# A group's four sums kept on one engine, one more group by seven products, and a small copy cut in 24

## The chip, the cores and the metric

The kernel runs on one core of a Trainium2 chip. A core has five engines that work side by side and wait for one another through semaphores: TensorE (PE) multiplies 128x128 tiles into PSUM, VectorE (DVE) and ScalarE (ACT) read PSUM and SBUF, GpSimd (POOL) works in SBUF, and SyncE (SP) issues most of the DMAs. The metric is the device time of one execution in microseconds (us). A difference of 0.2% (0.5 us here) is about what a measurement of this kernel can tell from no change.

## What is computed

`x` is 2 x 4000 x 512, everything in bfloat16. Two convolutions of five taps, each with a GELU and each keeping every second step, bring 4000 steps to 1000. Then follows the joint network:

```python
fe = jnp.einsum("btd,de->bte", f, w_f)      # 2 x 1000 x 512
ge = jnp.einsum("bud,de->bue", g, w_g)      # 2 x 8 x 512
j = jnp.tanh(fe[:, :, None, :] + ge[:, None, :, :])
return jnp.einsum("btud,dv->btuv", j, w_o)  # 2 x 1000 x 8 x 512
```

The last line is the large one: 16000 rows of `j`, each 512 long, times a 512 x 512 matrix.

## The kernel before

All work is first written down as a list of operations (`Plan.op`, `Plan.dma`), each with what it reads and writes. From overlaps of these the waits follow. Which engine runs which operation in which order is not computed in the kernel: the tables `ORDER["pe"]`, `["act"]`, `["dve"]`, `["pool"]` and `["sp"]` hold it, as differences between operation numbers. Each engine goes through its table from front to back, so an operation that has to wait holds up all that stands behind it on its engine. For some operations (`flex`) the table also decides the engine, which is whichever table holds the number.

The joint stage, from about 130 us to the end, cuts the 16000 rows into 125 tiles of 128 rows. `tanh` (ACT, L453) writes the rows of `j` into two rings, `jT` and `jX`. A tile is multiplied in one of two ways.

- `Plain`: four matmuls of 512 columns, one copy out of PSUM by ACT or DVE, one store.
- `Seven`: four neighbouring tiles are one group, taken as a 2x2 matrix of blocks times the 2x2 blocks of `w_o`, by Winograd's form of Strassen's scheme with seven block products in place of eight. A product is four matmuls of 256 columns, so a group has 28. Beforehand `sums` (L1094) makes four 128x512 sums of blocks of `j` in SBUF, numbered 0 to 3: sum 1 reads sum 0, and sum 3 reads sum 1. Products 5, 6, 7 and 3 use sums 0, 1, 2 and 3. Afterwards seven passes over PSUM bring the result out: three `keep` copies to SBUF (`sn`, L563 on ACT or L564 on DVE), three adds of a kept copy to PSUM, always on DVE (`og`, L448), and one copy `out4` (`og`, L563 or L564). The keep of product 1 must be done before product 6 goes to the same bank, and the add of product 7 before product 4 does.

The loop over `seven` puts products of two groups between each other: product 1 of group n, 7 of n-1, 5 and 2 of n, 6 of n, 4 of n-1, 3 of n. The sums of group n+1 are listed between 2 and 6. Of 125 tiles 28 groups take 112; 13 are `Plain`: two at the start, three at the end, and four pairs in gaps between later groups (`gaps`), each tile of a pair standing between two groups.

In the tables of before, the sums are split one by one: of 112 sums, 86 stand in POOL's table and 26 in DVE's. Twenty of 28 groups have at least one on DVE, none has all four there. `Plan.emit` adds one more kind of wait for these: an operation marked `port` on POOL waits for the nearest earlier marked one on DVE, where the planned starts lie within 1.5 us.

Two small things elsewhere matter. `NPRE` = 14 tiny ACT activations of one number (`warm`, L453) stand at the head of ACT's table; after them come ACT's first copies, of transposed input into `eo`. The first direct matmuls read `eo` and the first tap of `w1`; the following ones need the second tap from HBM. And `ge` (L1004 in the schedule) multiplies `g` by `w_g` into 64 columns of one bank, which a single ACT copy brings to `geT`; every tanh reads one column of it as its bias.

Of the kernel before, what the change touches and what calls it, by code (L numbers as in the profile page):

```python
# [7 lines left out]
ACT = mybir.ActivationFunctionType  # L8
# [6 lines left out]

ORDER = {
    "pe": """
# [13 lines left out]
        4 2 3""",  # L31
    "act": """
# [9 lines left out]
        3 12 7 1 8 1""",  # L42
    "dve": """
# [9 lines left out]
        7 6 17 67 -61 18 -37 46 35 -29 4 17 36 -10 3 -36 13 16 27 7 -21 27 15 -3 9 8 2""",  # L53
    "pool": """
        1 55 1 -55 1 1 1 28 218 1 -217 258 -252 253 8 89 174 150 1 54 -2 1 -31 33 33 2 -1 38 -36 35 40 -38 37 34 2 33
        -32 33 32 -30 31 1 1 33 1 28 1 1 28 155 -154 1 27 2 -1 33 -31 32 1 28 2 -1 31 -29 30 1 26 37 -36 37 1 1 33 34
        -33 34 -32 33 1 29 2 -1 33 2 -1 33 2 -1 35 2 -1 36 2 -1 28 -26 27 1 27 1 27 1 1""",
    "sp": """
        6 15 1 1 1 1 1 1 1 1 1 1 1 2 2 1 1 1 1 2 1 1 1 1 1 248 1 1 1 1 1 1 2 1 1 1 1 1 254 1 1 145 3 33 33 4 1 1 30 4 33
        4 1 1 33 4 31 4 1 1 29 4 29 4 1 1 29 4 25 4 1 1 25 4 25 4 1 1 27 4 27 4 1 1 25 4 25 4 1 1 19 1 11 4 21 11 4 19  # L60
        11 4 17 11 1 1 4 17 11 1 1 4 17 11 4 1 1 19 11 4 21 1 11 4 25 4 23 1 1 4 23 4 19 1 1 7 3 3 5 5""",
}


class View:


    __slots__ = ("ap", "cells", "psum")
# [42 lines left out]


class Op:
    __slots__ = ("eng", "fn", "reads", "writes", "dma", "signal", "count", "sem", "val", "idx", "cost", "pin", "after", "wire", "alt", "port", "slack")


class Plan:
# [12 lines left out]
    def op(self, eng, fn, reads=(), writes=(), cost=0.1):  # L130
        o = Op()
        o.eng, o.fn, o.dma, o.signal, o.idx, o.alt, o.port = eng, fn, False, False, len(self.ops), None, self.port
        o.reads, o.writes, o.cost, o.pin, o.after = tuple(reads), tuple(writes), cost, self.pin, list(self.hold)
        self.ops.append(o)
        return o
# [7 lines left out]
    def dma(self, eng, fn, reads=(), writes=(), sem=None, nbytes=524288, rate=330e3, slack=0.0):  # L143

        o = Op()
        o.eng, o.fn, o.dma, o.signal, o.idx, o.alt, o.port = eng, fn, True, False, len(self.ops), None, False
        o.reads, o.writes, o.cost, o.pin, o.after, o.wire = tuple(reads), tuple(writes), 0.43, True, [], nbytes / rate
        o.slack = slack
        if sem is None:
            sem = [self.nc.alloc_semaphore(f"s_d{o.idx}"), 0]  # L150
        sem[1] += 16
        o.sem, o.val = sem[0], sem[1]
        self.ops.append(o)
        return o
# [162 lines left out]
def bass_standalone__seq2seq_rnn_t_joint__speech_kernel(  # L317
# [22 lines left out]
    NK = D // P  # L340
# [12 lines left out]
    BU = B * U  # L353
    NT = 512
    NWARM = 8
    NPRE = 14
    TAPS = (0, 4, 2, 1, 3)
    NX = 2

    with ExitStack() as es:  # L360
        cur = [16512]
# [32 lines left out]
        geT = at("geT", [NK * BU], FP32)  # L394
# [3 lines left out]
        warm = at("warm", [2], FP32)  # L398
# [36 lines left out]
        ps = Psum(es.enter_context(nc.psum_tensor("acc", [P, 8 * NT], FP32)))  # L435
        block = es.enter_context(nc.Block(no_gpsimd_drain=True))
        pl = Plan(nc)
        sub, add = ALU.subtract, ALU.add
# [12 lines left out]
        def act(o, i, func, scale=1.0, bias=None):  # L451
            rd = (i,) if bias is None else (i, bias)
            pl.op("act", lambda e: e.activation(o.ap, i.ap, func, scale=scale,  # L453
                                                bias=0.0 if bias is None else bias.ap), rd, (o,),
                  o.ap.free_size() * 0.833e-3 + (0.05 if i.psum else 0.105 if bias is None else 0.186))
# [42 lines left out]
            return pl.dma("sp", lambda e: e.dma_start_transpose(out=dst.ap, in_=src), (), (dst,), nbytes=n * 2 * D, rate=175e3, slack=slack)  # L498

        came = [load_xr(0)]  # L500
        for _ in range(NPRE):
            act(warm[0:1], warm[1:2], ACT.Gelu_apprx_tanh)

        def load_w1(i, after=None):
            o = load_w("sp", w1_sb[i], w1[i].rearrange("(k c) d -> c k d", c=P), 0.5 if i == TAPS[1] else 0.2)
# [196 lines left out]
        class Unit:  # L702


            count = 0
# [108 lines left out]
        def ge():  # L814
            c0 = bank()
            for m in range(NK):
                mm(ps.cols(c0 + m * BU, BU), [(wg_sb[k, m * P:(m + 1) * P], gT[k]) for k in range(NK)], True, True)
            act(geT[:], ps.cols(c0, NK * BU), ACT.Copy)

        def fe(b, half, m):  # L820
            q = NT3 // 2
# [250 lines left out]
        class Seven:  # L1072
# [15 lines left out]
            def sums(self):  # L1088
                S = self.S
                eng = "dve" if self.n in (0, 1) else "pool"  # L1090
                pl.port = True
                for i, x, y, op in ((0, self.a(1, 0), self.a(1, 1), add), (1, S[0], self.a(0, 0), sub),
                                    (2, self.a(0, 0), self.a(1, 0), sub), (3, self.a(0, 1), S[1], sub)):
                    fn = lambda e, o=S[i], x=x, y=y, op=op: e.tensor_tensor(out=o.ap, in0=x.ap, in1=y.ap, op=op)  # L1094
                    alt = {"pool": (fn, 1.12), "dve": (fn, 0.34)}
                    pl.flex({k: alt[k] for k in (("dve", "pool"))}, (x, y), (S[i],))
                pl.port = False

            def product(self, i, bk, start, check=False):
# [125 lines left out]
        piece(4)  # L1225

        S1 = 15
        gaps = (1, 3, 5, 7)
        jts = [2 + 4 * i for i in range(S1)]
        j = 2 + 4 * S1  # L1230
        for n in range(13):
            jts.append(j)
            j += 4 + 2 * gaps.count(n)
        assert jts[-1] + 4 < ntile
# [72 lines left out]
```

## Time and profile before

| what | value |
|---|---|
| time, median of 3 runs | 250.3 us (250.1 to 250.35) |
| profiled execution, its own time | 250.55 us |
| its span | 248.7 us |
| PE busy in the span | 243.8 us (98%) |
| DVE busy | 208.0 us (84%) |
| ACT busy | 197.6 us (79%) |
| POOL busy | 100.7 us (41%) |
| granted clock of TensorE | 1.00 |

The span is what the profiler sees of the engines; the time holds 1.85 us more that lie around it. Matmuls overlap one another, so the pace of PE is read from the starts of neighbouring matmuls and not from the duration of one. An engine that is busy for 80% of the whole span can be full in one stage; the table by stage, below, shows which.

### The profile page before, as it was taken

Reading aid. Unit: us, or ns where it says so; the run is one execution under the profiler, and the core shown is the slowest. Engines: PE = TensorE matmul, PEld = TensorE weight load, DVE = VectorE, ACT = ScalarE, POOL = GpSimd, SP = SyncE. Lnnn points to the kernel's source line nnn. Section 1 sums busy time; section 2 is a strip of 40 time slices with the busy share of each in tenths; the row PEclk is TensorE's granted clock in tenths of the full one; section 3 lists DMA queues with packets and bytes.
Section 4 is the critical chain, followed back from the end, with each engine's and each line's share of the span. In section 5 each row is a group of like instructions: output and inputs, shape, how many; then the busy total and the mean of one; then the engine's idle time right before and its main releaser. Section 6 shows DMA issues by size and latency. Waiting matters only on the chain.

```text
span 248.7 us, 5271 instructions
## 1 busy us (share of the span) xinstructions
PE 243.8 (98%) x1938; PEld 182.6 (73%) x1944; DVE 208.0 (84%) x371; ACT 197.6 (79%) x349; POOL 100.7 (41%) x107
## 2 busy tenths in 40 slices
PE   7999999999999999999999999999999999999994
PEld 3879976666666666666566888777788878777883
DVE  1799996967999994796957889778999999996793
ACT  8787948458786475643699999999999999998672
POOL 1000000000000000000008988978799999999530
PEclk9999999999999999999999999999999999999999
DMA  6999999989000061000001043323345554454547
GB/s 212 319 224 179 126 209 173 193 169 355 31 3 0 0 209 48 0 4 0 0 3 42 31 147 106 100 87 127 109 156 161 172 188 162 160 182 137 192 153 249
DMA packets 54871, 31.83 MB, mean 128 GB/s; under 512 B 31902, under 2 KB 54590, under 8 KB 54846
## 3 DMA queue, kind: packets, MB, share of 16 engines
q1 hardware_dynamic: 54558, 31.34, 47.2%
q8 instruction: 15, 0.25, 0.5%
q10 hardware_dynamic: 288, 0.16, 0.2%
q14 instruction: 10, 0.08, 0.1%
HBM read 7.60 MB, written 16.38 MB: 96 GB/s over the span
## 4 chain that ended last, share of the span: by engine, by line
PE 86%; ACT 7%; DMA 2%; issue 1%; DVE 1%; SPq 0%; DVEq 0%; ACTq 0%
PE acc L461 86%; ACT jT L453 3%; DMA w_sb<-in_w_dram 2%; ACT sn L563 1%; ACT og L563 1%; ACT jX L453 1%; DVE og L448 1%; ACT sd L453 1%; DVE sn L564 0%; DVE og L564 0%; PE acc L599 0%; ACT fT L453 0%; SPq L479 0%; SPq L488 0%; ACT ost L453 0%
## 5 line engine op out<-in xcount | busy, mean ns | idle before, releaser
L448 DVE TENSOR_TENSOR og<-acc,sn 128x512 bf16<-128x512 f32 x84 | 54.7, 682 | 5.1 <-PE acc L461 5.1
L453 ACT ACTIVATE jT<-feT,geT 128x1000 bf16<-128x1000 f32 (+5 forms) x60 | 57.5, 1017 | 0.3 <-DVE feT L448 0.3
L1094 POOL TENSOR_TENSOR ss<-jT 128x512 f16<-128x512 bf16 x34 | 39.7, 1182 | 35.2 <-DVE ss L1094 33.3
L461 PE MATMUL acc<-tw,ss 128*128 128x256 f16 x336 | 46.0, 273 | 0.0
L461 PE MATMUL acc<-row,w_sb 128*128 128x334 bf16 (+2 forms) x224 | 39.2, 297 | 0.0
L461 PEld LDWEIGHTS acc<-tw,ss 128*128 128x128 f16 x336 | 32.3, 98 | 7.5 <-ACT sn L563 0.5
L461 PE MATMUL acc<-wo_sb,jT 128*128 128x256 bf16 (+1 forms) x205 | 33.1, 283 | 0.2
L563 ACT ACTIVATE sn<-acc 128x512 f32<-128x512 f32 x48 | 29.7, 628 | 3.4 <-PE acc L461 2.8
L564 DVE COPY sn<-acc 128x512 f32<-128x512 f32 x36 | 24.6, 685 | 6.3 <-PE acc L461 6.0
L453 ACT ACTIVATE hT<-acc 128x334 bf16<-128x334 f32 (+3 forms) x36 | 15.4, 430 | 17.4 <-PE acc L461 16.9
L461 PEld LDWEIGHTS acc<-row,w_sb 128*128 128x128 bf16 x224 | 21.2, 97 | 9.3 <-DVE acc L605 0.7
L453 ACT ACTIVATE sd<-acc 128x334 f32<-128x334 f32 (+2 forms) x48 | 20.5, 432 | 8.7 <-PE acc L461 7.4
L461 PEld LDWEIGHTS acc<-wo_sb,jT 128*128 128x128 bf16 x208 | 20.2, 98 | 5.1
L1094 POOL TENSOR_TENSOR ss<-ss,jT 128x512 f16<-128x512 f16 x19 | 22.3, 1179 | 2.4 <-DVE ss L1094 1.9
L445 POOL MEMSET hT<- 128x8 bf16 (+2 forms) x6 | 0.8, 148 | 55.5 <-ACT hT L453 43.0
L448 DVE TENSOR_TENSOR row<-row 128x1336 bf16<-128x1336 bf16 (+2 forms) x24 | 19.1, 806 | 0.0
L1094 POOL TENSOR_TENSOR ss<-jT,ss 128x512 f16<-128x512 bf16 x15 | 17.5, 1169 | 2.4 <-DVE ss L1094 2.4
L453 ACT ACTIVATE jX<-feT,geT 128x1000 bf16<-128x1000 f32 (+3 forms) x20 | 18.4, 965 | 0.0
L605 DVE SCALAR_TENSOR_TENSOR acc<-acc,sd 128x334 f32<-128x334 f32 (+2 forms) x24 | 11.7, 488 | 7.6 <-PE acc L461 7.5
L461 PE MATMUL acc<-xp,w_t 128*128 128x334 bf16 (+1 forms) x96 | 17.6, 305 | 0.0
L461 PE MATMUL acc<-hT,w_t 128*128 128x334 bf16 x96 | 17.6, 304 | 0.0
L461 PE MATMUL acc<-wo_sb,ss 128*128 128x256 bf16 x112 | 17.1, 273 | 0.0
(129 smaller groups left out, 473.4 us busy)
## 6 DMA issues: line engine op xcount, KB each, us to landing
out_dram<-og SPq DMA_DIRECT2D x42, 256.0 KB, 2.2
w_sb<-in_w_dram SPq DMA_DIRECT2D x10, 512.0 KB, 5.9
out_dram<-og SPq DMA_DIRECT2D x14, 128.0 KB, 2.3
out_dram<-ost SPq DMA_DIRECT2D x10, 128.0 KB, 1.9
xr<-in_x_dram SPq DMA_DIRECT2D x1, 512.0 KB, 3.2
wf_sb<-in_w_f_dram SPq DMA_DIRECT2D x1, 512.0 KB, 4.2
wg_sb<-in_w_g_dram SPq DMA_DIRECT2D x1, 512.0 KB, 5.2
wo_sb<-in_w_o_dram SPq DMA_DIRECT2D x1, 512.0 KB, 6.8
```

The lines of the kernel that those rows point to most:

```text
L445: pl.op("pool", lambda e: e.memset(v.ap, 0.0), (), (v,))
L448: pl.op(eng, lambda e: e.tensor_tensor(out=o.ap, in0=a.ap, in1=b.ap, op=op), (a, b), (o,), 0.02 + 2.14e-3 * o.ap.free_size() if eng == "po ...
L453: pl.op("act", lambda e: e.activation(o.ap, i.ap, func, scale=scale, bias=0.0 if bias is None else bias.ap), rd, (o,), o.ap.free_size() * ...
L461: ins = e.matmul(o.ap, lhsT=l.ap, rhs=r.ap, start=start and n == 0, stop=stop and n == len(pairs) - 1, skip_group_check=not check)
L563: pl.flex({"act": (lambda e: e.activation(o.ap, v.ap, ACT.Copy), 0.05 + n * 0.833e-3), "dve": (lambda e: e.tensor_copy(out=o.ap, in_=v.ap) ...
L564: "dve": (lambda e: e.tensor_copy(out=o.ap, in_=v.ap), 0.065 + n * 1.04e-3)}, (v,), (o,))
L605: pl.op(eng, lambda e: e.scalar_tensor_tensor(out=o.ap, in0=a.ap, scalar=f, in1=b.ap, op0=ALU.mult, op1=add), (a, b), (o,), vec_cost(o, (a ...
L1094: fn = lambda e, o=S[i], x=x, y=y, op=op: e.tensor_tensor(out=o.ap, in0=x.ap, in1=y.ap, op=op)
```

## The change

- `sums` no longer splits a group. Groups 0, 1, 4, 7, 10, 13, 16, 19, 22 and 25 (`ONV`) have all four sums on DVE, the other groups all four on POOL. The order within a group becomes 0, 2, 1, 3. On DVE the first sum also lists the other inputs of the group among its reads, so the group starts when all its data is there. (`glue` is set and read nowhere.)
- 29 groups in place of 28. They take 116 tiles, and 9 are `Plain`: two at the start, three at the end, two pairs in gaps.
- Thirteen of the 14 tiny activations go.
- The copy of `ge` to `geT` becomes 24 copies of two or three columns each.
- All five tables are new. From their running sums: the operations on PE go from 696 to 706, on ACT from 350 to 363, on DVE from 371 to 385, on POOL from 103 to 93, on SP from 138 to 137. DVE has 40 sums in place of 26, POOL 76 in place of 86. The copies that either engine could take go, on ACT, from 82 to 83 (keeps 51 to 58, `out4` 24 to 20, plain tiles 7 to 5; the keeps and outs of the second convolution's projection are counted in), on DVE from 47 to 46 (39 to 35, 4 to 9, 4 to 2). PE's table is the same through the tail; in the joint stage product 1 of the next group now often stands before product 4 of the last. The 24 pieces stand on ACT between the two last `fT` evictions before the joint stage (22 of them) and right behind (2). In DVE's table the blocks of four of seven groups are unbroken; in groups 7, 10 and 22 there stand 8, 13 and 19 other operations among the four. The blocks of groups 13, 16, 19 and 25 have the add of a product 7 right behind them.

```diff
-    NPRE = 14
+    ONV = (0, 1, 4, 7, 10, 13, 16, 19, 22, 25)
     TAPS = (0, 4, 2, 1, 3)
     NX = 2
+    NG = 24
...
-        for _ in range(NPRE):
-            act(warm[0:1], warm[1:2], ACT.Gelu_apprx_tanh)
+        act(warm[0:1], warm[1:2], ACT.Gelu_apprx_tanh)
...
-            act(geT[:], ps.cols(c0, NK * BU), ACT.Copy)
+            cut = [NK * BU * i // NG for i in range(NG + 1)]
+            for i, j in zip(cut, cut[1:]):
+                act(geT[i:j], ps.cols(c0 + i, j - i), ACT.Copy)
...
-                for i, x, y, op in ((0, self.a(1, 0), self.a(1, 1), add), (1, S[0], self.a(0, 0), sub),
-                                    (2, self.a(0, 0), self.a(1, 0), sub), (3, self.a(0, 1), S[1], sub)):
+                for i, x, y, op in ((0, self.a(1, 0), self.a(1, 1), add), (2, self.a(0, 0), self.a(1, 0), sub),
+                                    (1, S[0], self.a(0, 0), sub), (3, self.a(0, 1), S[1], sub)):
                     fn = lambda e, o=S[i], x=x, y=y, op=op: e.tensor_tensor(out=o.ap, in0=x.ap, in1=y.ap, op=op)
-                    alt = {"pool": (fn, 1.12), "dve": (fn, 0.34)}
-                    pl.flex({k: alt[k] for k in (("dve", "pool"))}, (x, y), (S[i],))
+                    if self.n in ONV:
+                        o = pl.op("dve", fn, (x, y) if i else (x, y, self.a(0, 0), self.a(0, 1)), (S[i],), 0.34)
+                        o.glue = i > 0
+                    else:
+                        pl.op("pool", fn, (x, y), (S[i],), 1.12)
...
-        gaps = (1, 3, 5, 7)
+        gaps = (1, 5)
         jts = [2 + 4 * i for i in range(S1)]
         j = 2 + 4 * S1
-        for n in range(13):
+        for n in range(14):
             jts.append(j)
             j += 4 + 2 * gaps.count(n)
```

More of the change, by code (lines that the diff above doesn't have):

```diff
@@ L17 @@
     "pe": """
[2 rows of a table removed]
[2 rows of a table added]
         1 -9 1 12 1 5 1 23 1 4 1 2 1 2 1 6 2 1 4 1 2 1 2 1 2 2 1 4 1 2 1 2 1 16 2 1 4 1 2 1 2 1 18 2 1 4 1 2 1 2 1 18 2
         1 4 1 2 1 2 1 14 2 1 4 1 2 1 2 1 10 2 1 4 1 2 1 2 1 5 2 1 4 1 2 1 2 1 6 2 1 4 1 2 1 2 1 2 2 1 4 1 2 1 2 1 6 7 1
[2 rows of a table removed]
[2 rows of a table added]
         2 6 1 2 1 3 1 3 1 4 1 2 1 2 1 2 1 2 1 8 1 2 1 3 1 5 1 6 1 2 1 2 1 2 1 2 1 6 1 2 1 3 1 3 6 1 2 1 2 1 2 1 2 6 1 2
         1 3 1 5 4 1 2 1 2 1 2 1 2 6 1 2 1 3 1 3 4 1 2 1 2 1 2 1 2 6 1 2 1 3 1 5 4 1 2 1 2 1 2 1 2 6 1 2 1 3 1 5 1 2 1 2
[5 rows of a table removed]
-        4 2 3""",
-    "act": """
[9 rows of a table removed]
-        3 12 7 1 8 1""",
-    "dve": """
[9 rows of a table removed]
-        7 6 17 67 -61 18 -37 46 35 -29 4 17 36 -10 3 -36 13 16 27 7 -21 27 15 -3 9 8 2""",
[5 rows of a table added]
+        2 1 3 1 3 1 2 1 2 1 2 1 2 1 2 1 8 1 -4 1 6 3 3 1 4 2 3""",
+    "act": """
[9 rows of a table added]
+        -52 53 30 -50 51 -38 -57 67 -65 71 -40 50 3 12 6 -69 79 3 8 6 10 3 10 6 10 11 6 6 15 7 1 8 1""",
+    "dve": """
[9 rows of a table added]
+        3 -27 40 -24 17 23 7 1 1 1 21 -40 15 16 29 7 -21 27 16 7 6 10 4 7 6 6 9 -3 9 8 2""",
     "pool": """
-        1 55 1 -55 1 1 1 28 218 1 -217 258 -252 253 8 89 174 150 1 54 -2 1 -31 33 33 2 -1 38 -36 35 40 -38 37 34 2 33
-        -32 33 32 -30 31 1 1 33 1 28 1 1 28 155 -154 1 27 2 -1 33 -31 32 1 28 2 -1 31 -29 30 1 26 37 -36 37 1 1 33 34
-        -33 34 -32 33 1 29 2 -1 33 2 -1 33 2 -1 35 2 -1 36 2 -1 28 -26 27 1 27 1 27 1 1""",
+        1 42 1 -42 1 1 1 15 218 1 -217 258 -252 253 8 89 174 226 1 1 35 -34 33 77 -75 74 -73 75 33 -32 33 1 66 -65 66 1
+        33 -32 33 1 1 57 2 1 -2 28 2 -1 2 61 98 -96 -1 2 28 1 1 64 -63 65 34 -33 34 1 56 -55 56 1 35 -34 33 66 -64 97
+        -96 62 33 -31 33 -32 33 57 1 1 54 -53 24 1 1 28 -27 28 1""",
     "sp": """
-        6 15 1 1 1 1 1 1 1 1 1 1 1 2 2 1 1 1 1 2 1 1 1 1 1 248 1 1 1 1 1 1 2 1 1 1 1 1 254 1 1 145 3 33 33 4 1 1 30 4 33
-        4 1 1 33 4 31 4 1 1 29 4 29 4 1 1 29 4 25 4 1 1 25 4 25 4 1 1 27 4 27 4 1 1 25 4 25 4 1 1 19 1 11 4 21 11 4 19
-        11 4 17 11 1 1 4 17 11 1 1 4 17 11 4 1 1 19 11 4 21 1 11 4 25 4 23 1 1 4 23 4 19 1 1 7 3 3 5 5""",
+        6 2 1 1 1 1 1 1 1 1 1 1 1 2 2 1 1 1 1 2 1 1 1 1 1 248 1 1 1 1 1 1 2 1 1 1 1 1 254 1 1 168 3 33 33 4 1 1 30 4 33
+        4 1 1 33 4 31 4 1 1 29 4 29 4 1 1 29 4 25 4 1 1 25 4 25 4 1 1 27 4 27 4 1 1 25 4 25 4 1 1 19 1 11 4 21 11 4 25 4
+        25 1 1 4 19 11 4 1 1 17 11 4 27 1 1 4 27 4 25 1 1 4 25 4 23 1 1 4 23 4 19 1 1 7 3 3 5 5""",
 }
@@ L113 @@
 class Op:
-    __slots__ = ("eng", "fn", "reads", "writes", "dma", "signal", "count", "sem", "val", "idx", "cost", "pin", "after", "wire", "alt", "port", "slack")
+    __slots__ = ("eng", "fn", "reads", "writes", "dma", "signal", "count", "sem", "val", "idx", "cost", "pin", "after", "wire", "alt", "port", "slack", "glue")
 class Plan:
@@ L132, in op @@
         o.eng, o.fn, o.dma, o.signal, o.idx, o.alt, o.port = eng, fn, False, False, len(self.ops), None, self.port
+        o.glue = False
         o.reads, o.writes, o.cost, o.pin, o.after = tuple(reads), tuple(writes), cost, self.pin, list(self.hold)
@@ L146, in dma @@
         o.eng, o.fn, o.dma, o.signal, o.idx, o.alt, o.port = eng, fn, True, False, len(self.ops), None, False
+        o.glue = False
         o.reads, o.writes, o.cost, o.pin, o.after, o.wire = tuple(reads), tuple(writes), 0.43, True, [], nbytes / rate
```

54 rows, old and new, of the table ORDER are left out of this document.

## The prediction

> **What bounds the kernel now.** I read the page's head first, then a table by stage, then the list of what the weight loads waited for, since these show where TensorE really stood still.
>
> ```profile
> span 248.7 us, 5271 instructions
> PE 243.8 (98%) x1938; PEld 182.6 (73%) x1944; DVE 208.0 (84%) x371; ACT 197.6 (79%) x349; POOL 100.7 (41%) x107
> ```
>
> The table's columns are the stretch, then busy time of PE, PEld, DVE, ACT and POOL, the granted clock and the DMA share.
>
> ```profile
> 130.00:150.00 20.00, 19.95 (x159) 15.43 (x159) 16.24 (x29) 20.00 (x30) 17.33 (x16) 1.00 0.24 79
> 150.00:170.00 20.00, 20.00 (x158) 15.26 (x157) 15.96 (x28) 20.00 (x30) 16.89 (x15) 1.00 0.29 93
> 170.00:190.00 20.00, 20.00 (x173) 16.30 (x172) 19.33 (x31) 20.00 (x33) 18.39 (x18) 1.00 0.42 138
> 190.00:210.00 20.00, 19.89 (x172) 16.62 (x172) 19.55 (x33) 20.00 (x30) 20.00 (x18) 1.00 0.56 180
> 210.00:227.00 17.00, 16.89 (x140) 13.47 (x141) 15.89 (x26) 17.00 (x28) 17.00 (x16) 1.00 0.50 163
> 227.00:243.00 16.00, 15.95 (x141) 13.41 (x140) 12.63 (x22) 10.81 (x20) 8.72 (x8) 1.00 0.50 162
> ```
>
> PE is full through the whole joint stage. So is ACT until 227 us, POOL from 190 to 227, and DVE has only 0.67, 0.45 and 1.11 us left between 170 and 227: four engines are near their limit at once. The waits of the weight loads say which one gives the pace.
>
> ```profile
> PEld acc L461 <- ACT eo L453: 0.9, 1, 0.9
> PEld acc L461 <- DVE acc L605: 0.7, 3, 0.2
> PEld acc L461 <- ACT sn L563: 0.5, 2, 0.3
> PEld acc L461 <- DMA w_sb<-in_w_dram: 0.3, 1, 0.3
> ```
>
> In the joint stage only two waits appear, together 0.5 us, both for an ACT keep; none is for POOL. So TensorE's own stream sets the end, and what the other engines do costs time only where it makes TensorE wait.
>
> **The change part by part.** *One group more.* A group of seven products takes 28 matmuls of 256 columns where four plain tiles take 16 of 512. Their pace is in the starts.
>
> ```profile
> 132.65 1.02 PE L461 MATMUL acc<-wo_sb,jT 128*128 128x512 bf16 x4
> 133.52 0.73 PE L461 MATMUL acc<-row,w_sb 128*128 128x334 bf16 x4
> ...
> 205.26 0.60 PE L461 MATMUL acc<-tw,jX 128*128 128x256 f16 x4
> 205.70 0.60 PE L461 MATMUL acc<-wo_sb,ss 128*128 128x256 bf16 x4
> ```
>
> Four matmuls of 512 columns take 133.52 - 132.65 = 0.87 us, four of 256 take 0.44. Four plain tiles are 4 x 0.87 = 3.48 us, a group is 7 x 0.437 = 3.06 (unrounded: 0.435 to 0.44). The gain is 0.41 us on the path that sets the end. PE's order around it costs nothing more as long as each wait is covered.
>
> *Who makes the sums.* The durations, smallest/median/largest:
>
> ```profile
> L1094 POOL TENSOR_TENSOR ss<-jT x34: 1147/1157/1339, 131.0 to 228.9; 128x512 f16<-128x512 bf16 x34
> L1094 DVE TENSOR_TENSOR ss<-jT x9: 409/431/925, 130.5 to 178.3; 128x512 f16<-128x512 bf16 x9
> L1094 DVE TENSOR_TENSOR ss<-jT,ss x8: 418/842/1442, 153.2 to 232.6; 128x512 f16<-128x512 bf16 x8
> L1094 DVE TENSOR_TENSOR ss<-jX x4: 415/546/1469, 186.0 to 234.5; 128x512 f16<-128x512 bf16 x4
> ```
>
> POOL gets 76 sums in place of 86: 10 x 1.157 = 11.6 us less. That buys no time by itself, since TensorE never waited for POOL. DVE gets 40 in place of 26. The same sum takes 0.41 us or up to 1.47 there, and the long ones meet a POOL sum:
>
> ```profile
> 178.31 0.93 DVE L1094 TENSOR_TENSOR ss<-jT 128x512 f16<-128x512 bf16 x1
> ...
> 177.80 1.16 POOL L1094 TENSOR_TENSOR ss<-jT 128x512 f16<-128x512 bf16 x1 [0.89 <-DVE og L448]
> ```
>
> DVE's sum ends at 179.24, about 0.3 us behind the end of POOL's at 178.96. The joint stage's DVE rows, with busy time and mean, give the present load and its idle time:
>
> ```profile
> L448 DVE TENSOR_TENSOR og<-acc,sn 128x512 bf16<-128x512 f32 x84 | 54.7, 682 | 5.1 <-PE acc L461 5.1
> L564 DVE COPY sn<-acc 128x512 f32<-128x512 f32 x36 | 24.6, 685 | 6.3 <-PE acc L461 6.0
> L1094 DVE TENSOR_TENSOR ss<-jT,ss 128x512 f16<-128x512 bf16 x8 | 6.9, 863 | 0.0
> L1094 DVE TENSOR_TENSOR ss<-jT 128x512 f16<-128x512 bf16 x9 | 4.8, 543 | 1.3 <-ACT jT L453 1.3
> L1094 DVE TENSOR_TENSOR ss<-jX 128x512 f16<-128x512 bf16 x4 | 3.0, 744 | 0.0
> L1094 DVE TENSOR_TENSOR ss<-ss,jT 128x512 f16<-128x512 f16 x4 | 2.4, 602 | 0.0
> L1094 DVE TENSOR_TENSOR ss<-jX,ss 128x512 f16<-128x512 bf16 x1 | 0.8, 792 | 0.0
> ```
>
> That is 6.9 + 4.8 + 3.0 + 2.4 + 0.8 = 17.9 us for 26, a mean of 0.69, so 0.28 of waiting each. After the change 40 sums are 40 x 0.41 = 16.4 us without any waiting; seven unbroken blocks have one start each that can meet POOL and the three broken ones up to three, 16 in all, at 0.28: 4.5 us. I take 20.9, so +3.0 us; the bounds are -1.5 (no meeting) and +9.7 (all 40 at the mean of now). Three adds more are 3 x 0.68 = 2.0, one copy fewer -0.7. DVE gets +4.3 us, against 5.1 + 6.3 + 1.3 = 12.7 us idle in these rows, of which 2.2 lie between 170 and 227. Four blocks (16, 19, 22, 25) fall there, and before 170 most of the idle time. ACT has one copy more, 0.63 us by its mean of 628 ns. What this costs TensorE lies between nothing and some 3 us (worked out with the first rival); in the likeliest case I take nothing, because the idle time is as long as the addition.
>
> The Trainium skill, "SBUF — State Buffer", section "Who interferes with whom", states that VectorE with two SBUF inputs and a reading GpSimd instruction exclude each other, and whoever issues first holds the port for its whole instruction. The pair of rows at 178 us agrees; by that rule each of the 16 starts can wait a whole POOL sum of 1.16 us, so that DVE's sums would take up to 16.4 + 18.6 = 35.0 us in place of 20.9.
>
> *The two old waits for ACT keeps.* They stand here:
>
> ```profile
> 178.51 0.33 PEld L461 LDWEIGHTS acc<-tw,ss 128*128 128x128 f16 x4 [0.26 <-ACT sn L563]
> ...
> 187.80 0.33 PEld L461 LDWEIGHTS acc<-tw,ss 128*128 128x128 f16 x4 [0.19 <-ACT sn L563]
> ```
>
> Both are product 6 behind the keep of product 1, and the new order starts product 1 earlier in several groups of just this stretch. Bounds: 0 to 0.45 us gained; I take 0.2.
>
> *The head.* ACT's thirteen tiny activations end before its `eo` copies:
>
> ```profile
> 2.03 3.25 ACT L453 ACTIVATE warm<-warm 128x1 f32<-128x1 f32 x14
> ...
> 5.18 1.55 ACT L453 ACTIVATE eo<-acc 128x256 bf16<-128x256 bf16 x3
> 5.88 1.65 PEld L461 LDWEIGHTS acc<-eo,w_sb 128*128 128x128 bf16 x16 [0.86 <-ACT eo L453]
> ...
> 7.86 1.64 PEld L461 LDWEIGHTS acc<-eo,w_sb 128*128 128x128 bf16 x16 [0.33 <-DMA w_sb<-in_w_dram]
> ```
>
> The filler runs until 5.28, so `eo` may come some 0.4 us earlier and the first 16 matmuls too. But at 7.86 TensorE waits for the second tap's weights, whose DMA nothing here moves; the 0.86 us wait shrinks and the 0.33 us wait grows. Zero.
>
> *The 24 pieces.* They stand on ACT where it is idle:
>
> ```profile
> 115.70 0.22 ACT L453 ACTIVATE geT<-acc 128x64 f32<-128x64 f32 x1
> 116.85 0.45 ACT L453 ACTIVATE fT<-acc 128x334 bf16<-128x334 f32 x1 [0.93 <-PE acc L461]
> 119.97 0.45 ACT L453 ACTIVATE fT<-acc 128x334 bf16<-128x334 f32 x1 [2.67 <-PE acc L461]
> ```
>
> No copy of two columns is in the trace. Above, the tiny activations, each waiting for the one before, come every 3.25 / 14 = 0.232 us: 24 would be 5.6 us. Below, if only columns counted, they'd cost what the one copy does, 0.22. Independent copies overlap, so I take nearer the lower: about 0.06 each, an estimate, 1.4 us, which the 2.67 us gap covers. If it did not, ACT would come late to the tanhs of 122 to 131 us and TensorE would wait for them there.
>
> *Sum.* The profiled execution took 250.55 us (span 248.7 and 1.85 around it), 0.25 above the median of 250.3. 250.55 - 0.41 - 0.2 = 249.94; on the median that is **249.7 us**.
>
> **The rivals.**
> - *DVE eats the saving.* The added 4.3 us spread evenly puts 57/113 of it, 2.2 us, into 170 to 227, exactly the idle time there; each further 0.1 us is a wait. For: ACT is at 20.00 of 20 beside it. Against: DVE has sums in those 57 us now too (its rows run from 130.5 to 234.5 us), so the addition there may be smaller. I take 0.4 us of waits, four blocks at 0.1: 250.3 - 0.41 + 0.4 = 250.3.
> - *A block stands in front of the add that product 4 needs.* This one ends slower. Place: groups 13, 16, 19 and 25, with the add of a product 7 right behind the block. If the block starts as product 7 ends, the add is done 4 x 0.41 + 0.68 = 2.3 us later, while TensorE has products 5, 2 and 6, 3 x 0.437 = 1.3, or 1.75 with the next product 1. It waits 0.6 to 1.0 us each time. For: DVE is nearly full there. Against: blocks needn't start so late, their results are due only with the next group but one or later. It decides from 0.9 us in all, two such blocks: 250.3 - 0.4 + 1.6 = 251.5.
> - *POOL slips in between the four.* Then each of the 40 can meet a POOL sum as the 26 do now, and the +9.7 us hold: 9.7 + 2.0 - 0.7 = 11.0, half of it less 2.2 idle is 3.3 us short, of which I let 0.6 go to ACT after 227: 250.3 - 0.4 + 2.7 = 252.6. For: the four wait for one another, and each start is open. Against: POOL's marked sums wait for DVE's. By the rule of "SBUF — State Buffer" in the Trainium skill, at its worst, the 35.0 us would make DVE short by another 3.7 us, half of what 35.0 is over 27.6.
> - *The pieces cost 0.232 us each.* 5.6 less 2.67 and 0.93 idle is 2.0 us late: 251.9.
> - *Nothing gained:* the end could hang on something else than TensorE. The chain of waits ends with TensorE up to 245.6 us, so I give this no chance of its own.
>
> **How the numbers follow.** Saving holds: 0.50, own range 249.2 (with all of 0.45 us of waits and 0.25 elsewhere gained) to 249.8. DVE eats it: 0.27, 249.8 to 250.8. Block before the add: 0.13. POOL slips in: 0.05. Pieces: 0.05. Faster by over 0.2% (below 249.8) 0.50, within 0.2% 0.27, slower 0.23. The range is 249.1 to 251.2: it leaves out most of the last three cases' upper ends, some 0.15, and little below.
>
> **What would show it.** PE: 16 matmuls of 512 columns fewer and 28 of 256 more; the last matmul ends about 0.6 us earlier. POOL: 76 sums, about 88 us, with gaps. DVE: 40 sums, a mean near 0.52 us; 0.41 would say no meeting, 0.69 that POOL slips in. In the weight loads' waits, entries for DVE `og` before product 4 mean the second rival; entries for ACT `jT` near 131 us the pieces. The head's wait for the DMA grows to about 0.7 us. The prediction is wrong if waits of TensorE in the joint stage exceed 0.5 us.

## The result, and the profile after

The changed kernel takes 251.69 us (median; 251.27 to 252.19), the kernel before 250.88 us on the same chip (250.1 to 251.55). The ratio is 1.0036 [1.0026, 1.0045]: slower by 0.36%, where 249.7 us and a gain had been forecast. The kernel before read 0.58 us more here than the 250.3 from which the forecast was worked out, so the differences are what to compare: 0.6 us less forecast, 0.81 us more measured. The profiled execution took 251.99 us, 1.44 more than that of before; what that is above 0.81 lies within the spread of single executions (250.1 to 251.55 for the kernel before), and the account that follows is of these two executions.

The head of the page, with the shares of the chain that ended last (the chain is followed back from the last instruction, at each step to what released it); below it the same line of the kernel before:

```profile
span 250.2 us, 5311 instructions
...
PE 244.5 (98%) x1952; PEld 184.5 (74%) x1956; DVE 216.9 (87%) x385; ACT 199.6 (80%) x362; POOL 90.2 (36%) x97
...
PE 87%; DVE 7%; DMA 3%; issue 1%; ACT 1%; SPq 0%; DVEq 0%
```

```profile
PE 86%; ACT 7%; DMA 2%; issue 1%; DVE 1%; SPq 0%; DVEq 0%; ACTq 0%
```

POOL fell by 10.5 us (11.6 had been forecast), DVE rose by 8.9 where 4.3 were forecast, and 7% of the chain runs through DVE in place of 1%. The waits of the weight loads, in the same columns as in the prediction, tell why:

```profile
PEld acc L464 <- DVE og L451: 1.3, 2, 0.7
PEld acc L464 <- DVE sn L566: 1.1, 2, 0.6
PEld acc L464 <- DMA w_sb<-in_w_dram: 1.0, 2, 0.7
...
PEld acc L464 <- DVE acc L607: 0.5, 1, 0.5
PEld acc L464 <- ACT sn L565: 0.3, 2, 0.2
```

The first two entries are new, 2.4 us on DVE's adds and keeps. The timeline of the weight loads gives their places in the joint stage:

```profile
139.01 0.77 PEld L464 LDWEIGHTS acc<-tw,ss 128*128 128x128 f16 x8 [0.58 <-DVE sn L566]
...
185.17 0.33 PEld L464 LDWEIGHTS acc<-tw,ss 128*128 128x128 f16 x4 [0.19 <-ACT sn L565]
185.66 0.11 PEld L464 LDWEIGHTS acc<-wo_sb,ss 128*128 128x128 f16 x2 [0.15 <-ACT sn L565]
189.43 0.33 PEld L464 LDWEIGHTS acc<-tw,jT 128*128 128x128 bf16 x4 [0.60 <-DVE og L451]
196.17 0.33 PEld L464 LDWEIGHTS acc<-tw,jT 128*128 128x128 bf16 x4 [0.73 <-DVE og L451]
208.63 0.77 PEld L464 LDWEIGHTS acc<-tw,ss 128*128 128x128 f16 x8 [0.54 <-DVE sn L566]
```

Four waits of 0.54 to 0.73 us. What TensorE itself loses is read from the starts of its matmuls:

```profile
194.90 0.60 PE L464 MATMUL acc<-tw,ss 128*128 128x256 f16 x4
195.34 0.38 PE L464 MATMUL acc<-wo_sb,jT 128*128 128x256 bf16 x2
196.17 0.61 PE L464 MATMUL acc<-tw,jT 128*128 128x256 f16 x4 [0.45 <-DVE og L451]
```

Four matmuls take 195.34 - 194.90 = 0.44 us, so the two at 195.34 would let the next start at 195.56. It starts at 196.17: 0.61 lost. Counted so, TensorE stands still in the joint stage for 0.47 + 0.50 + 0.62 + 0.44 us at the four waits and 0.13 at the two ACT keeps, 2.17 us in all before rounding; before it was 0.29 us. From the first matmul that uses the second tap to the last one of the kernel it is 237.74 us before and 239.13 after, +1.39. Of that span TensorE stood still for 0.66 before and 2.49 after, +1.83; so the stream itself became shorter by 0.44. The saving of the 29th group is there, and four waits, 2.03 us, take back more than four times as much. (The span grew by 1.47 us: 1.39 of this, 0.23 by which the second tap's first matmul started later, less 0.15 behind the last matmul.)

Each wait follows a block of four sums on DVE: groups 1, 13, 16 and 19. This is DVE's timeline at group 13, and POOL's:

```profile
186.25 0.78 DVE L1098 TENSOR_TENSOR ss<-jT 128x512 f16<-128x512 bf16 x2
186.95 1.37 DVE L1098 TENSOR_TENSOR ss<-ss,jT 128x512 f16<-128x512 f16 x1
188.35 0.42 DVE L1098 TENSOR_TENSOR ss<-jT,ss 128x512 f16<-128x512 bf16 x1
188.69 1.88 DVE L451 TENSOR_TENSOR og<-acc,sn 128x512 bf16<-128x512 f32 x3
```

```profile
185.25 1.16 POOL L1098 TENSOR_TENSOR ss<-jT 128x512 f16<-128x512 bf16 x1
186.83 1.21 POOL L1098 TENSOR_TENSOR ss<-jT,ss 128x512 f16<-128x512 bf16 x1 [0.42 <-DVE ss L1098]
```

The third sum of the block takes 1.37 us in place of 0.41. POOL had waited 0.42 us for DVE's first sum of this block, was let go by it, and began at 186.83, just ahead of 186.95. DVE's sum ends at 188.32, 0.28 behind the end of POOL's at 188.04. The first of the three adds behind the block, which frees the bank of product 4, comes about 1 us late, and TensorE waits for it at 189.43. At groups 1 and 19 an inner sum is likewise hit by a POOL sum that was let go by the first sum of the block; at group 16 it is one that stands in the plan 0.15 us ahead of the block and waits for no sum of it. A hit alone doesn't make a wait: the block of group 25 is hit as well, and TensorE doesn't wait behind it.

```profile
230.12 1.75 DVE L1098 TENSOR_TENSOR ss<-jT 128x512 f16<-128x512 bf16 x2
```

The durations (smallest/median/largest) of the sums on DVE that read `jT` show how common hits are:

```profile
L1098 DVE TENSOR_TENSOR ss<-jT x16: 411/436/1396, 132.4 to 230.5; 128x512 f16<-128x512 bf16 x16
...
L1098 DVE TENSOR_TENSOR ss<-ss,jT x8: 411/822/1376, 133.1 to 231.8; 128x512 f16<-128x512 f16 x8
L1098 DVE TENSOR_TENSOR ss<-jT,ss x8: 424/425/425, 133.6 to 232.2; 128x512 f16<-128x512 bf16 x8
```

`ss,jT` is the third of the four on DVE, an inner one in unbroken blocks: half of these eight are at 0.82 us or longer. In the unbroken blocks the last sum never was hit.

### The profile page after: what moved, and what is told of

Its sections match the earlier page's. It is cut to its first block, busy times and chain, and to the rows that moved or that the text cites. A ratio compares the mean times of both kernels' runs of the same rounds, so it can differ in the third digit from the quotient of the medians.

```text
span 250.2 us, 5311 instructions
## 1 busy us (share of the span) xinstructions
PE 244.5 (98%) x1952; PEld 184.5 (74%) x1956; DVE 216.9 (87%) x385; ACT 199.6 (80%) x362; POOL 90.2 (36%) x97
## 4 chain that ended last, share of the span: by engine, by line
PE 87%; DVE 7%; DMA 3%; issue 1%; ACT 1%; SPq 0%; DVEq 0%
PE acc L464 87%; DVE og L451 4%; DMA w_sb<-in_w_dram 3%; DVE ss L1098 2%; DVE sn L566 1%; ACT jX L456 0%; ACT og L565 0%; ACT sn L565 0%; PE acc L601 0%; SPq L482 0%; SPq L491 0%; ACT ost L456 0%; DVE og L566 0%; DVEq L280 0%
## 5 line engine op out<-in xcount | busy, mean ns | idle before, releaser
L451 DVE TENSOR_TENSOR og<-acc,sn 128x512 bf16<-128x512 f32 x87 | 56.1, 684 | 1.6 <-PE acc L464 0.9
L456 ACT ACTIVATE jT<-feT,geT 128x1000 bf16<-128x1000 f32 (+5 forms) x60 | 56.9, 993 | 0.0
L1098 POOL TENSOR_TENSOR ss<-jT 128x512 f16<-128x512 bf16 x28 | 32.7, 1173 | 46.9 <-ACT sn L565 37.9
L464 PE MATMUL acc<-tw,ss 128*128 128x256 f16 x348 | 47.7, 273 | 0.6 <-DVE sn L566 0.6
L464 PEld LDWEIGHTS acc<-tw,ss 128*128 128x128 f16 x348 | 33.4, 98 | 7.6 <-DVE sn L566 1.1
L565 ACT ACTIVATE sn<-acc 128x512 f32<-128x512 f32 x55 | 33.2, 617 | 3.6 <-PE acc L464 3.3
L566 DVE COPY sn<-acc 128x512 f32<-128x512 f32 x32 | 21.9, 686 | 1.4 <-PE acc L464 1.2
L1098 POOL TENSOR_TENSOR ss<-jT,ss 128x512 f16<-128x512 bf16 x16 | 19.1, 1198 | 3.0 <-DVE ss L1098 2.1
L1098 POOL TENSOR_TENSOR ss<-ss,jT 128x512 f16<-128x512 f16 x16 | 18.9, 1184 | 2.3 <-DVE ss L1098 1.3
L464 PE MATMUL acc<-wo_sb,ss 128*128 128x256 bf16 x116 | 17.7, 273 | 0.0
```

The lines of the kernel that those rows point to most:

```text
L451: pl.op(eng, lambda e: e.tensor_tensor(out=o.ap, in0=a.ap, in1=b.ap, op=op), (a, b), (o,), 0.02 + 2.14e-3 * o.ap.free_size() if eng == "po ...
L464: ins = e.matmul(o.ap, lhsT=l.ap, rhs=r.ap, start=start and n == 0, stop=stop and n == len(pairs) - 1, skip_group_check=not check)
L565: pl.flex({"act": (lambda e: e.activation(o.ap, v.ap, ACT.Copy), 0.05 + n * 0.833e-3), "dve": (lambda e: e.tensor_copy(out=o.ap, in_=v.ap) ...
L566: "dve": (lambda e: e.tensor_copy(out=o.ap, in_=v.ap), 0.065 + n * 1.04e-3)}, (v,), (o,))
```

## The experiments

Five theories were put against each other. A: a POOL sum slips in between the four of a DVE block. B: the block alone, by where it stands, makes the add or keep behind it late. C: the 24 pieces and the missing tiny activations cost the time. D and E came up with the later runs: D, that a fetch of ACT's instructions costs time when the number of instructions makes it fall beside the last stores; E, that fewer tiny activations cost time at the head. All kernels keep the order of the tables of the kernel that they start from; where operations go or come, only the numbers shift. Ratios are against the kernel before, run beside them.

**POOL waits for the last sum of a block.** `near` is the nearest earlier sum on DVE; a POOL sum now waits for the last of that sum's unbroken block.

```diff
+        glued = {a: b for a, b in zip(order["dve"], order["dve"][1:]) if ops[b].glue}
+        def last(i):
+            while i in glued:
+                i = glued[i]
+            return i
...
-                o.after.append(near)
+                o.after.append(last(near))
```

> The changed kernel, where a POOL sum that waits for the first or an inner sum of an unbroken DVE block waits for the last sum of that block. In the changed kernel's profile four waits of TensorE of 0.44 to 0.62 us (2.03 in all) follow the blocks of groups 1, 13, 16 and 19; in each block one inner sum takes 1.37 us beside a POOL sum that began in the middle of the block. Theory A (POOL slips in): the waits behind groups 1, 13 and 19 go, 1.41 us, and the one behind 16 stays, because its POOL sum is planned before the block and doesn't wait; time 1.4 us below the changed kernel, ratio to the kernel before 0.998. Theory B (the block's place alone: 4 x 0.41 + 0.68 us stand in front of the pass that TensorE needs): the waits stay at 0.4 us or more each, ratio 1.003. Theory C (pieces and missing tiny activations): ratio unchanged at 1.0036.

Measured: 252.0 us, 1.0049 [1.0032, 1.0066], not faster. The waits behind groups 1, 13 and 19 are gone, but the one behind group 16 is the longest of all. DVE, POOL and the weight load of this kernel there:

```profile
192.72 1.91 DVE L1105 TENSOR_TENSOR ss<-jX 128x512 f16<-128x512 bf16 x2
194.56 1.37 DVE L1105 TENSOR_TENSOR ss<-ss,jX 128x512 f16<-128x512 f16 x1
```

```profile
193.01 1.34 POOL L1105 TENSOR_TENSOR ss<-jX 128x512 f16<-128x512 bf16 x1
194.31 1.34 POOL L1105 TENSOR_TENSOR ss<-jT,ss 128x512 f16<-128x512 bf16 x1
```

```profile
197.04 0.33 PEld L471 LDWEIGHTS acc<-tw,jT 128*128 128x128 bf16 x4 [1.54 <-DVE og L458]
```

Two POOL sums, sum 0 of group 17 and sum 3 of group 15, hit two sums of it, and the block takes 3.7 us in place of 1.5. Both are planned ahead of the block (1.27 and 0.15 us) and run 3.5 and 3.7 us later than planned, where the block starts 1.9 later. New waits of 0.55 and 0.27 appear at 147 us, behind the block of group 4, of which two sums are hit in this kernel, and 0.75 at 60 us, behind an input that landed late. So the rule holds off only what is planned behind the block; POOL sums that are late run into it.

**Also those planned shortly ahead.** A POOL sum planned up to 0.9 us ahead of a block waits for the end of the block as well.

```diff
+            soon = [b for b in firsts if 0 < self.start[b] - self.start[o.idx] < 0.9]
+            if soon:
+                o.after.append(last(soon[0]))
+            elif near is not None and self.start[near] > self.start[o.idx] - 1.5:
+                o.after.append(last(near))
```

> As the run before, and a POOL sum planned to begin up to 0.9 us before a block waits for the block's end too (groups 4, 16 and 25). Theory A: the wait behind group 16 (0.62 us) goes as well, in all 2.0 us below the changed kernel, ratio to the kernel before 0.996; that would be the 0.41 us of the one group more and the two old waits that did not come back. Theory B: ratio 1.003 or more, since POOL loses time and nothing is won. Theory C: 1.0036.

Measured: 250.99 us, 1.002 [1.0004, 1.0035]. Two waits are left, 0.56 behind group 16, where sum 0 of group 17 slipped in, and 0.77 behind group 19, where sum 3 of group 18 did.

**The pieces alone.** The kernel before, with one tiny activation and 24 pieces.

```diff
-    NPRE = 14
+    NPRE = 1
+    NG = 24
...
-            act(geT[:], ps.cols(c0, NK * BU), ACT.Copy)
+            cut = [NK * BU * i // NG for i in range(NG + 1)]
+            for i, j in zip(cut, cut[1:]):
+                act(geT[i:j], ps.cols(c0 + i, j - i), ACT.Copy)
```

> The kernel before, with 1 tiny activation in place of 14 and the copy to geT in 24 pieces at the same place of ACT's order; nothing else is changed. Theories A and B: no difference, ratio 0.9985 to 1.0015; the pieces come 0.053 us apart as in the changed kernel, 1.3 us in a gap of 2.67 us. Theory C: the head or the pieces cost 0.5 us or more, ratio 1.002 or above.

Measured: 251.12 us, 1.0019 [1.0003, 1.0035]. ACT, DVE and the weight loads of the changed kernel itself show what a part of it is:

```profile
115.77 1.55 ACT L456 ACTIVATE geT<-acc 128x3 f32<-128x3 f32 x22
116.95 0.71 ACT L456 ACTIVATE fT<-acc 128x334 bf16<-128x334 f32 x1
```

```profile
117.69 0.68 DVE L451 TENSOR_TENSOR sf<-fT 128x1008 bf16<-128x1008 bf16 x1 [0.37 <-ACT fT L456]
118.29 0.51 DVE L607 SCALAR_TENSOR_TENSOR acc<-acc,sd 128x334 f32<-128x334 f32 x1
```

```profile
118.85 0.40 PEld L464 LDWEIGHTS acc<-row,w_sb 128*128 128x128 bf16 x4 [0.47 <-DVE acc L607]
```

The copy `fT` behind the 22 pieces ends at 117.66; in the kernel before it ended at 116.85 + 0.45 = 117.30, by the rows of the prediction (about 0.08 of the difference is that all work here lies later). DVE's sum of `fT` waits for it, the operation behind that is late, and TensorE stands still for 0.16 us (0.29 in the kernel with the pieces alone). Kernels without pieces show no such standstill. That is 0.06 to 0.12% of the time; the rest of the 0.19%, if it isn't chance, stays open.

**Everything but the pieces.** The changed kernel with 14 tiny activations and one copy.

```diff
-        act(warm[0:1], warm[1:2], ACT.Gelu_apprx_tanh)
+        for _ in range(14):
+            act(warm[0:1], warm[1:2], ACT.Gelu_apprx_tanh)
...
-            for i, j in zip(cut, cut[1:]):
-                act(geT[i:j], ps.cols(c0 + i, j - i), ACT.Copy)
+            act(geT[:], ps.cols(c0, NK * BU), ACT.Copy)
```

> The changed kernel with 14 tiny activations and one copy to geT again; sums, groups and all orders are as changed. Theories A and B: as the changed kernel, ratio to the kernel before 1.0036 within 0.0015. Theory C: the loss goes, ratio 1.000 or below.

Measured: 251.62 us, 1.0041 [1.0027, 1.0055]. TensorE loses 0.47, 0.53, 0.62 and 0.44 us at the same four places, and nothing near 119 us. So the loss is in the sums; C falls as its main cause.

**The two that still slipped in, held.** To the kernel of the second experiment, two waits are added by hand: sum 0 of group 17 behind the block of group 16, sum 3 of group 18 behind that of group 19.

```diff
+        holds = {self.tag[a]: self.tag[b] for a, b in (((17, 0), (16, 3)), ((18, 3), (19, 3)))}
...
+            if o.idx in holds:
+                o.after.append(holds[o.idx])
+                continue
```

> As the second run (held, also those planned early), and the two POOL sums that still came into a block there, sum 0 of group 17 into block 16 and sum 3 of group 18 into block 19, wait for the last sum of these blocks. In the second run TensorE waited 0.45 and 0.67 us behind just these two blocks. Theory A (POOL slips in): no wait of 0.3 us or more is left in the joint stage, waits there sum to 0.3 us or less against 2.2 in the changed kernel; time 1.9 us below the changed kernel, ratio to the kernel before 0.996 to 1.000. Theory B (place of the block alone): waits of 0.4 us behind blocks 16 and 19 stay; ratio 1.002.

Measured: 250.21 us, 0.9983 [0.9967, 0.9998]. The joint stage loses 0.48 us of TensorE in five small pieces, none above 0.21. Not every hit is gone: sum 0 of group 20 now runs into the block of group 19.

**The same without pieces**, with 14 tiny activations and one copy (both edits above together).

> The run above with 14 tiny activations and one copy to geT. In the runs with pieces TensorE waited 0.16 to 0.29 us at 119 us behind a DVE operation, in those without it didn't. Theory A: another 0.2 us, ratio 0.996 to 0.999, the fastest of all; theory B: 1.001.

Measured: 249.77 us, 0.9967 [0.995, 0.9984]. This beats both kernels. Its page, then its waits of weight loads, then DVE and POOL at the block of group 13:

```profile
span 248.0 us, 5303 instructions
...
PE 244.2 (98%) x1956; PEld 184.9 (75%) x1956; DVE 214.9 (87%) x385; ACT 199.6 (81%) x352; POOL 88.7 (36%) x97
```

```profile
PEld acc L480 <- ACT sn L582: 0.7, 4, 0.2
...
PEld acc L480 <- DVE sn L583: 0.3, 1, 0.3
```

```profile
185.28 0.78 DVE L1113 TENSOR_TENSOR ss<-jT 128x512 f16<-128x512 bf16 x2
185.99 0.41 DVE L1113 TENSOR_TENSOR ss<-ss,jT 128x512 f16<-128x512 f16 x1
186.44 0.42 DVE L1113 TENSOR_TENSOR ss<-jT,ss 128x512 f16<-128x512 bf16 x1
186.78 1.88 DVE L467 TENSOR_TENSOR og<-acc,sn 128x512 bf16<-128x512 f32 x3
```

```profile
184.29 1.16 POOL L1113 TENSOR_TENSOR ss<-jT 128x512 f16<-128x512 bf16 x1
187.01 1.16 POOL L1113 TENSOR_TENSOR ss<-jT,ss 128x512 f16<-128x512 bf16 x1 [1.56 <-DVE ss L1113]
```

POOL waits 1.56 us in place of 0.42, the third sum takes 0.41, and the adds begin 1.50 us behind the start of the block in place of 2.44. The block stands in the same place of the table with the same add behind it, and TensorE doesn't wait: B falls for this block, and likewise for those of groups 1 and 16, whose inner sums take 0.41 to 0.42 us here. At group 19 a hit is left, in the first two sums, and TensorE loses 0.20 us behind that block, in place of 0.44 in the changed kernel. The block is hardly shorter (2.87 us in place of 2.98), so what else made the loss smaller there is not shown:

```profile
200.33 2.07 DVE L1113 TENSOR_TENSOR ss<-jX 128x512 f16<-128x512 bf16 x2
```

```profile
206.25 0.77 PEld L480 LDWEIGHTS acc<-tw,ss 128*128 128x128 f16 x8 [0.32 <-DVE sn L583]
```

This kernel differs from the kernel with everything but the pieces in POOL's waits alone, 1.0041 against 0.9967, some 0.7% or 1.9 us, each measured beside the kernel before. A is carried by that, and POOL, 36% busy, has the time to wait.

**One tiny activation, nothing else.** The kernel before with `NPRE` = 1.

```diff
-    NPRE = 14
+    NPRE = 1
```

> The kernel before with 1 tiny activation in place of 14, geT in one copy. If the 0.2% of the run with both came from the pieces, ratio 0.9990 to 1.0010 and no wait at 119 us; if it came from the head, 1.002.

Measured: 251.28 us, 1.0028 [1.0015, 1.0041]: slower, and at the end of the kernel. ACT's queue in the timeline of the tail:

```profile
245.50 1.84 ACTq L1039 DMA_DIRECT2D out_dram<-og  x1
...
247.75 0.34 ACTq L1039 DMA_DIRECT2D out_dram<-ost  x1
```

In the kernel before the first of these store issues took 0.38 us; here it is 1.84, and the end lies 3.96 us behind the last matmul in place of 3.13. It is the 449th instruction of ACT in the trace (counted from 0), before it was the 462nd, and the last packet of q14, a queue that loads instructions, starts at 245.82 us, in place of 238.42 (on the timeline's clock). That this packet is ACT's is inferred: it moves with the number of ACT's instructions. So D was put: a fetch that falls beside the last issues is waited for.

**Four tiny activations.** `NPRE` = 4 makes the issue the 452nd.

> The kernel before with 4 tiny activations. With 1 the profile showed ACT's next-to-last DMA issue taking 1.84 us in place of 0.38, as the 449th instruction of ACT's queue, beside an instruction fetch at 245.6 us; with 14 it is the 462nd and the fetch stands at 238.2. Theory D (where the fetch falls): with 4 it is the 452nd, so the fetch comes some instructions before the last stores, the issue takes 0.38 us and the ratio to the kernel before is 0.9990 to 1.0010. Theory E (fewer tiny activations cost at the head, the more the fewer): ratio 1.0015 or above, with the loss before 20 us.

Measured: 250.7 us, 1.0003 [0.9985, 1.0021]; issue 0.38 us, last fetch at 242.77 us, end 3.12 behind the last matmul. That is as D has it. It doesn't exclude E, whose 1.0015 lies inside the interval; the run with six, below, speaks against E.

**The held kernel with three tiny activations**, which makes the issue the 449th there.

```diff
-        for _ in range(14):
+        for _ in range(3):
             act(warm[0:1], warm[1:2], ACT.Gelu_apprx_tanh)
```

> The fastest kernel so far (changed kernel, POOL held out of the blocks, one copy to geT, 14 tiny activations) with 3 tiny activations, so that its first DMA issue at the end is the 449th of ACT's queue. Theory D: the issue takes 1.8 us, the end comes 0.9 us later, ratio 0.35% above that kernel's 0.9967, that is 1.000. Theory E: 0.1% above at most.

Measured: 251.04 us, 0.9998 [0.9982, 1.0013]. The issue took 1.23 us, but the end lay only 0.25 us further behind the last matmul. Most of this trace's 1.7 us more of span comes from inputs that landed late: the second tap's first matmul starts 0.23 us later than in the kernel with 14, and TensorE loses 1.19 us at 61 us. POOL's copy of a late input is the start of the latter:

```profile
57.60 0.26 POOL L563 COPY xp<-xe 128x16 bf16<-128x16 bf16 x1 [21.03 <-DMA xe<-in_x_dram]
```

In the kernel with 14 it starts at 54.29. The times of this run fit both D and chance, and the last experiment takes them up again.

**One slip put back.** The held kernel (14 tiny, one copy), with sum 3 of group 14 waiting for the first sum of group 13 again and not for the last.

```diff
+            if o.idx == self.tag[14, 3]:
+                o.after.append(near)
+                continue
```

> The fastest kernel so far, where sum 3 of group 14 on POOL waits for the first sum of block 13 again, as in the changed kernel. Theory A: one inner sum of block 13 takes 1.37 us again, TensorE waits about 0.5 us before a product 4 at 188 us, and the time is 0.5 us longer, ratio 0.9987 against 0.9967. Theory B: the waits stay as they are.

Measured: 250.82 us, 0.9994 [0.998, 1.0007]. The wait is back at its place, and no other is new in the joint stage. DVE and weight loads:

```profile
186.31 1.37 DVE L1116 TENSOR_TENSOR ss<-ss,jT 128x512 f16<-128x512 f16 x1
```

```profile
188.80 0.33 PEld L483 LDWEIGHTS acc<-tw,jT 128*128 128x128 bf16 x4 [0.63 <-DVE og L470]
```

TensorE loses 0.52 us there. That is 0.2%, and the ratio moved by 0.27%; a late input (0.49 us at 60 us in this trace) may be the rest. One wait of one POOL sum makes or unmakes a quarter of what TensorE lost.

**Six and three tiny activations in the held kernel**, run side by side.

```diff
-        for _ in range(14):
+        for _ in range(6):
             act(warm[0:1], warm[1:2], ACT.Gelu_apprx_tanh)
```

> The kernel with all GpSimd sums held and one copy of the second projection, with 6 tiny activations ahead (14 in the held kernel without pieces at 0.9967, 3 in the one at 0.9998). ACT's first store issue in the tail is then its instruction 452, as in the kernel before with 4 tiny activations. Theory D (only the place of ACT's instruction fetch at the tail counts): the issue takes 0.38 us, as it did with 14 and with 4, and the ratio is 0.996 to 0.998. Theory E (fewer tiny activations cost time at the head, whatever the tail does): the ratio is 0.999 or more with an issue of 0.38 us. A third reading, that the 0.9967 was helped by luck in when the input DMAs landed, would also show as 0.998 to 1.000 here, with waits for DMAs near 6, 8 and 60 us in the trace.

> The kernel with 3 tiny activations once more, beside the one with 6 on the same chip. Its earlier trace had a store issue of 1.23 us but also 2.4 us of waits for input DMAs and for what follows them near 6, 8 and 61 us, so that its 0.9998 could be either. Theory D: the store issue takes 1.2 to 1.8 us again, the end lies 0.2 to 0.9 us later behind the last matmul, and the ratio is 0.1 to 0.3% above that with 6 tiny activations. Theory E or luck with DMAs: both ratios are equal within 0.1%.

Measured: with six 249.98 us, 0.9971 [0.996, 0.9981], issue 0.38 us; with three 250.34 us, 0.999 [0.998, 1.0001], issue 1.34 us and the end 0.33 us further behind the last matmul:

```profile
244.73 1.34 ACTq L1059 DMA_DIRECT2D out_dram<-og  x1
```

D's issue time came in all three kernels where the issue is the 449th (1.84, 1.23, 1.34 us) and in none where it is the 452nd or later (0.38). In time the difference is 0.19%, with intervals that touch; the end explains 0.33 of the 0.36 us. E forecast 0.999 or more with six, and falls. The gain of the held kernel came again with six (0.9971), so it wasn't luck with the inputs.

## Why the prediction was wrong

**One group more: right.** 0.41 us were forecast, 0.44 found in the stream.

**Who makes the sums: here it failed.** The step is the one that takes nothing for TensorE "because the idle time is as long as the addition". Two things in it were wrong. The addition was mis-sized: sums on DVE went from 17.9 to 25.9 us by their groups, a mean of 0.65 in place of the 0.52 that 16 meetings gave, because inner sums of unbroken blocks met POOL too. Five did, at groups 1, 13, 16, 19 and 25, each at 1.37 us or a little more in place of 0.41. That is 4.8 us, and the forecast 20.9 was exceeded by 5.0. And 4.3 us of work were set against 12.7 us of idle time as sums, though no idle time can be used once a block has begun: a sum that is hit delays the add or keep behind it by about 1 us at once, and where that one is due, as behind four of the five, TensorE waits, however idle DVE is elsewhere. The held kernel (14 tiny activations, one copy) shows both: its sums take 23.2 us, still more than the 20.9 forecast, and yet cost TensorE only the 0.20 us behind group 19. Its ratio of 0.9967 is near the 0.998 (249.7 over 250.3) that was forecast for the change.

The Trainium skill, "SBUF — State Buffer", section "Who interferes with whom", calls the shared port an exclusive lock, and says of VectorE's two-port modes that whoever issues first has it for its whole instruction. The sums here show it, in the main, for a `tensor_tensor` with two SBUF inputs: of the 1.37 us of the hit sum, 1.09 lie beside what was left of POOL's sum (186.95 to 188.04), so DVE's sum didn't end before POOL's had. The rest is 0.28, less than the 0.41 that the sum takes alone, so a part of it went on meanwhile.

**The rivals.** "POOL slips in between the four" was the mechanism, at 0.05. It was priced by how full DVE is (252.6 us), and its counter-argument was, at three of the four places, the cause: "POOL's marked sums wait for DVE's". They wait for the nearest earlier one. At groups 1, 13 and 19 that was the first of the block, so that wait lets POOL go at the worst moment; at group 16 the POOL sum was planned ahead of the block and waited for nothing. "A block stands in front of the add that product 4 needs" had the victims at two of the four waits, groups 13 and 16, their size (0.60 and 0.73 us) and a loss near the measured one (251.5 is 1.2 us above its base of 250.3). That the loss came so near is in part luck: it was priced without hits for two blocks, and the block of group 13 with 4 x 0.41 us does no harm in the same place. All four waits stand behind a block with a hit inside. The two had been given as alternatives, each unlikely, when they were the two halves of one mechanism. Groups 1 and 19 wait for a keep on DVE, which neither named.

**The two old waits for ACT keeps.** They were 0.26 + 0.19 and became 0.19 + 0.15: 0.11 us gained, not 0.2.

**The head.** As forecast, nothing gained: the first matmul that reads `eo` starts 0.14 us earlier (5.74 in place of 5.88; 0.4 had been said), and the wait for the second tap's weights grew to 0.70 us, as was said. These weights landed 0.23 us later in this execution, which no run ties to the change.

**The 24 pieces.** The pitch was right (1.55 us for 22 with their overlap, 0.05 apart; 0.06 had been estimated). The cover was not: the gap of 2.67 us lies behind the next `fT`, and that `fT`, with what DVE makes of it, stood behind the pieces. It cost 0.16 us.

**What was to show it.** "The prediction is wrong if waits of TensorE in the joint stage exceed 0.5 us": those of the weight loads came to 2.8, and the mean of 0.65 was near the 0.69 named for POOL slipping in.

## What to carry to other kernels

Work moved onto an engine with spare time is not free because the idle time is long enough in sum: look at what stands right behind the moved block and who waits for it, and price one bad meeting there. If another engine contends for something with a run of short operations, make it wait for the last of the run; a wait for the first lets it go into the middle. Hold off what is planned just ahead of the run as well, since it may come late: the first hold alone gave 1.0049, no gain.

## What the runs showed of the hardware

The number of instructions on an engine can cost time at the far end of a kernel. An ACT store issue that is the engine's 449th instruction in the trace took 1.23 to 1.84 us, the same issue as the 452nd to 473rd 0.38, and the last packet of q14 lay within 0.5 us of it in the first case and 2 us or more ahead in the others. What the issue waited for is not in the trace; that it is the fetch follows from place and time alone. The Trainium skill, "Runtime: NRT & Kernel Launch", section "Instruction fetch mechanics", calls the cost of crossing a fetch boundary mostly hidden. If the fetch is the cause, it wasn't hidden here: the end came 0.25 to 0.83 us later.
